# Batch 0 of a fused attention and two-layer kernel: its own states loaded first, products of the identity, another order of the plan

## The chip, the cores and the metric

One core of a Trainium2 chip. The metric is device time in microseconds; the time of a kernel is the median of its runs. Matrix products run on TensorE (PE), elementwise work on VectorE (DVE), ScalarE (ACT) and GpSimd (POOL); transfers are issued from the queues of SyncE (SP) and ScalarE.

## The reference

```python
# x (8, 8, 512, 64), state (8, 8, 32, 64), w_in (512, 2048), w_out (2048, 512)
scores  = x @ state.T / 8;  a  = softmax(scores);  xread = a  @ state
scores2 = state @ x.T / 8;  a2 = softmax(scores2); sread = a2 @ x
y = concat([xread, sread], axis=2)          # per batch 512 token rows and 32 state rows
y = y.transpose(0, 2, 1, 3).reshape(4352, 512)
h = y @ w_in
g = where(h > 0, h, exp(min(h, 0)) - 1)     # ELU
out = g @ w_out
```

The weights arrive as 64-bit floats and are turned into 32-bit ones on the core.

## The kernel before

Eight batches run one after the other, then the state rows of all of them. Batches 1 to 7 form g from M = (states times w_in) and the softmax, sixteen feature blocks each, and multiply g by w_out in a form with fewer products (`Strassen`), while the attention of the next batch is woven in. Batch 0 is different: in it the weights are still arriving and being converted. Its steps stand in `plan`, an order written out by hand, and PE, SP, ACT, DVE and POOL each keep the order in which the plan names their instructions. From batch 1 on DVE, ACT and POOL may be reordered by the scheduler.

The names of the plan, with the engine of each; g counts two halves of the heads, k the weight blocks, f the sixteen feature blocks of 128:

- `kT` (PE) transposes the states, `kTc` (DVE) copies them to `kT`, which every product with states reads.
- `x:b.i` (PE) transposes half of x, `xc:b.i` (ACT) copies it. `sc:b` (PE) are the scores, 16 records, in banks 6 and 7.
- Softmax over tokens: `mx` (DVE) maximum, `ae` (ACT) exponential, `sd` (DVE) reciprocal of the sum, `sT` (PE) transposition, `sTc` (ACT) its copy, `sr` (PE) product with x, `src` (ACT) scaled copy.
- Softmax over states: `tr` (DVE) transposes the scores, `tm` (DVE) maximum, `ps` (POOL) subtraction, `te` (ACT) exponential, `su` (DVE) sum and reciprocal, `pm` (POOL) multiplication, `tt` (DVE) transposition to `aT`.
- `w:k.1` (ACT, three instructions) and `w:k.2` (DVE, four) convert weight block k of 32; blocks 0 to 3 are the first quarter of w_in, 4 to 7 the second, 8 to 11 the first quarter of w_out, 12 to 15 the third of w_in, 16 to 19 w_out, 20 to 23 w_in, 24 to 31 w_out.
- `M:0.c.h` (PE) is half a quarter of M, `Mc` (ACT) its copy; `M:1.0` and `Mc:1.0` are those of batch 1.
- `F:f` (PE) is h for block f, in bank 4 or 5; `R:f` (ACT) its exponential, `E:f` (DVE) writes g; `O:f` (PE) adds g times w_out to banks 0 to 3. At the end ACT and DVE copy these banks to `o_sb`; batch 1's third F goes to bank 3 when DVE has emptied it.

`kT`, `x`, `sc`, `M`, `sT` and `sr` all use banks 6 and 7, each after the copy of the one before. A product in 32-bit floats leaves two records on PE, a transposition one.

`fetch` issues the load of the next weight block, 512 KB, on SP. It is called six times ahead of the plan, once at `kTc` and then at the end of each `w:k.2`; after the last block it loads x of batch 1. A load waits until its place in `work` is free, eleven places that the weight blocks, the states `s_sb` and the transposed probabilities share in turn. The eight semaphores of the loads are also used in turn, so that a ninth load waits for the first to land:

```python
raw_states = load_states()          # eight loads, four on SP, four on ACT
load_x(0, [sync, scalar])           # four loads of 256 KB
for k in range(NRAW - 1):           # NRAW = 7
    fetch()
```

All instructions but a few are recorded at line 100, the helper through which the engines are called, and are told apart by their tiles.

Of the kernel before, what the change touches and what calls it, by code (L numbers as in the profile page):

```python
# [10 lines left out]
FP32 = mybir.dt.float32  # L11
# [14 lines left out]
def kernel(  # L26
# [15 lines left out]
    B, H, S, D = x.shape  # L42
    NS = state.shape[2]
    DM, DF = moe_w_in.shape
    P = 128
    R = S // P
    NP = H // 2
    G = 2
# [4 lines left out]
    NRAW = 7  # L53
# [11 lines left out]
    def pool(name, bufs, **kw):  # L65
        return ctx.enter_context(tc.tile_pool(name=name, bufs=bufs, **kw))

    cpool = pool("const", 1)
# [4 lines left out]
    work = pool("work", NRAW + 4)  # L73
# [11 lines left out]
    def bank(i):  # L85
        return psum[:, i]

    def pair(i):

        return psum[:, i : i + 2]  # L90
# [3 lines left out]
    class InOrder:  # L94
# [10 lines left out]
    tensor, sync, vector, scalar, gpsimd = (  # L105
        InOrder(e) for e in (nc.tensor, nc.sync, nc.vector, nc.scalar, nc.gpsimd)
    )
    matmul = tensor.matmul

    def transpose(out, in_):  # L110


        for t in range(2):
            rows = slice(t * 64, (t + 1) * 64)
            tensor.transpose(out[:, t], in_[rows], ident[rows, rows], tile_position=(t * 64, 0))
# [4 lines left out]
    ident = cpool.tile([P, P], FP32, name="ident")  # L120
# [6 lines left out]
    kT = cpool.tile([P, B, P], FP32, name="kT")  # L127
# [3 lines left out]
    x_t, st, m_t = {}, {}, {}  # L131

    def load_x(b, engines):
        x_t[b] = xpool.tile([P, R, DM], FP32, name="x_sb")
        x_v = x[b].rearrange("h (p r) d -> p r h d", r=R)
        for r in range(R):
            engines[r % len(engines)].dma_start(
                out=x_t[b][:, r].rearrange("p (h d) -> p h d", d=D), in_=x_v[:, r]
            )

    def load_states():
        raw = work.tile([P, B, G, D], FP32, tag="w", name="s_sb")
        s_v = state.rearrange("b (m c) n d -> m c n b d", c=G)
        for m in range(NP):
            for c in range(G):
                (sync, scalar)[c].dma_start(out=raw[m * NS : (m + 1) * NS, :, c], in_=s_v[m, c])
        return raw

    def turn_states(raw):
        ps = st["k_ps"] = pair(6).rearrange("p t (b q) -> p t b q", q=64)  # L150
        for b in range(B):
            transpose(ps[:, :, b], raw[:, b].rearrange("p c d -> p (c d)"))

    def load_weights(src):
        _, n, k = src.shape
        raw = work.tile([P, n, k], moe_w_in.dtype, tag="w", name="raw")
        sync.dma_start(out=raw, in_=src)
        return raw
# [39 lines left out]
    def load_w_in(c, k):  # L198

        h, n = divmod(k, 2)  # L200
        rows = slice(2 * n, 2 * n + 2)
        cols = slice(c * 512 + h * 256, c * 512 + (h + 1) * 256)
        return w_in[:, 2 * c + h, rows], load_weights(w_in_v[:, rows, cols])

    def load_w_out(fo):
        raw = load_weights(w_out_v[:, fo : fo + 1])
        return w_out[:, fo : fo + 1], raw
# [178 lines left out]
    def max_part(fo, e, ps):  # L386
        vector.scalar_tensor_tensor(
            out=g_all[:, fo, : ps.shape[-1]], in0=e, scalar=-1.0, in1=ps,
            op0=ALU.add, op1=ALU.max,
        )  # L390
# [247 lines left out]
    shape = [P, 3, FO // 4, P]  # L638
# [50 lines left out]
    def first_batch():  # L689

        plan = """
            kT kTc x:0.0 xc:0.0 w:0.1 x:0.1 xc:0.1 w:0.2 w:1.1 sc:0 mx:0.1 w:2.1 tr:0.1 tr:0.0
            tm:0.1 w:3.1 tm:0.0 ps:0.1 mx:0.0 w:1.2 ps:0.0 ae:0.1 ae:0.0 te:0.1 sT:0 sd:0.0 sd:0.1
            te:0.0 su:0.1 sTc:0 su:0.0 pm:0.1 w:4.1 M:0.0.0 w:3.2 pm:0.0 Mc:0.0.0 w:7.1 sr:0 tt:0.1
            tt:0.0 w:4.2 F:0 src:0 w:8.1 w:2.2 F:1 R:0 w:5.1 E:0 M:0.0.1 w:8.2 Mc:0.0.1 R:1 F:2  # L700
            w:5.2 w:9.1 O:0 E:1 w:10.1 w:9.2 R:2 F:3 w:10.2 w:6.1 M:0.1.0 O:1 E:2 Mc:0.1.0 w:6.2 R:3
            w:12.1 E:3 F:4 w:7.2 w:11.1 O:2 w:12.2 w:13.1 R:4 w:11.2 M:0.1.1 F:5 w:14.1 w:13.2 O:3
            R:5 Mc:0.1.1 E:4 w:16.1 E:5 w:14.2 F:6 w:17.1 M:0.2.0 w:16.2 F:7 R:6 w:15.1 E:6 O:4
            w:17.2 Mc:0.2.0 w:18.1 w:15.2 F:8 R:7 w:18.2 O:5 w:21.1 E:7 R:8 w:21.2 M:0.2.1 w:19.1
            O:6 E:8 w:23.1 w:19.2 Mc:0.2.1 F:9 w:23.2 w:24.1 O:7 w:25.1 w:24.2 w:20.1 w:25.2 F:10
            R:9 O:8 w:20.2 w:22.1 E:9 R:10 w:22.2 M:0.3.0 w:26.1 F:11 E:10 O:9 Mc:0.3.0 w:26.2 R:11
            w:27.1 E:11 M:0.3.1 w:29.1 w:27.2 F:12 O:10 R:12 w:29.2 Mc:0.3.1 w:30.1 E:12 F:13 w:31.1
            w:30.2 O:11 R:13 w:31.2 w:28.1 E:13 x:1.0 w:28.2 F:14 xc:1.0 x:1.1 R:14 F:15 xc:1.1 E:14
            sc:1 R:15 O:12 mx:1.0 mx:1.1 ae:1.0 tr:1.0 ae:1.1 tr:1.1 tm:1.0 sT:1 tm:1.1 ps:1.0 O:13
            sd:1.0 sTc:1 sd:1.1 E:15 ps:1.1 te:1.0 su:1.0 te:1.1 pm:1.0 su:1.1 sr:1 pm:1.1 tt:1.0  # L710
            O:14 src:1 tt:1.1 M:1.0 O:15 Mc:1.0
        """.split()
        make_identity(nc, ident)
        o_ps = [bank(c) for c in range(R)]
        order = [lambda k=k: load_w_in(0, k) for k in range(4)]
        for c in range(1, FC + 1):
            if c < FC:
                order += [lambda c=c, k=k: load_w_in(c, k) for k in range(4)]
            order += [lambda fo=fo: load_w_out(fo) for fo in range(4 * c - 4, 4 * c)]
        w, h, e = [], {}, {}  # L720

        def fetch():
            if len(w) < len(order):
                w.append(order[len(w)]())
            elif 1 not in x_t:
                load_x(1, [sync])
                for c in range(FC):
                    k = slice(2 * c, 2 * c + 2)
                    sync.dma_start(out=w_in_mem[:, k], in_=w_in[:, k])

        raw_states = load_states()
        load_x(0, [sync, scalar])
        for k in range(NRAW - 1):
            fetch()
        groups = {
            "mx": column_max, "tr": turn_scores, "ae": column_exp, "tm": row_max,
            "ps": row_subtract, "te": row_exp, "su": row_sum, "pm": row_scale,
            "tt": turn_tokens, "sd": column_total,
        }
        whole = {  # L740
            "sc": scores, "sT": turn_state, "sTc": copy_state, "sr": state_read,
            "src": keep_read,
        }
        for step in plan:
            name, _, num = step.partition(":")
            num = [int(i) for i in num.split(".") if i]
            if name == "kT":
                turn_states(raw_states)
            elif name == "kTc":
                vector.tensor_copy(out=kT.rearrange("p b (t q) -> p t b q", t=2), in_=st["k_ps"])  # L750
                fetch()
            elif name in groups:
                groups[name](*num)
            elif name in whole:
                whole[name](*num)
            elif name == "w":
                (convert_1, convert_2)[num[1] - 1](*w[num[0]])
                if num[1] == 2:
                    fetch()
            elif name == "F":  # L760
                h[num[0]] = ffn1(0, num[0])
            elif name == "R":
                e[num[0]] = exp_part(h[num[0]])
            elif name == "E":
                max_part(num[0], e[num[0]], h[num[0]])
            elif name == "O":
                ffn2_row(o_ps, num[0])
            elif name == "x":
                turn_x(*num)
            elif name == "M":  # L770
                make_m(*num)
                if len(num) == 2:
                    make_m(1, 1, first=4)
            elif name == "xc":
                copy_x(*num)
            else:
                assert name == "Mc", step
                if len(num) == 3:
                    copy_half(*num)
                else:  # L780
                    for g in range(G):
                        copy_m(*num, g, scalar.copy)
        for g in range(G):
            copy_m(1, 1, g, scalar.copy)
        for i in range(2):
            o_sb = opool.tile([P, 2, DM], FP32, tag="o", name="o_sb")
            for c in range(2):
                (scalar.copy, vector.tensor_copy)[c](out=o_sb[:, c], in_=o_ps[2 * i + c])
            store(0, i, o_sb)
# [90 lines left out]
```

## Time and profile before

| | us |
|---|---|
| median of 5 runs | 763.6 |
| lowest, highest | 763.21, 764.36 |
| the profiled execution | 764.36 |
| its span | 762.5 |
| busy in the span: PE, DVE, ACT, POOL | 730.2, 467.1, 312.2, 35.1 |
| chain that ended last | PE 90%, DVE 6%, DMA 1%, ACT 1% |

The times in a trace count from the start of the span. A line of the timeline merges neighbouring instructions of one form: start, time that they took together, engine, tiles (out<-in), shapes, number, and in brackets the idle time of the engine before them with what ended it. A line of the windows gives a stretch, its length, busy time and instructions of PE, PEld (weight loads), DVE, ACT and POOL, the granted share of the PE clock, the busy share of the DMA engines and their GB/s.

### The profile page before, as it was taken

The numbers are of one execution on the slowest core, as the hardware profiler recorded it, in microseconds if no ns is written. First come the engines' busy times: TensorE is split into PE (matmuls) and PEld (weight loads), VectorE is DVE, ScalarE is ACT, GpSimd is POOL, SyncE is SP. The second block draws the span as 40 slices with busy tenths as digits, with TensorE's granted clock in tenths as the row PEclk, the third lists the DMA queues.
The fourth block names the chain that finished last, engine by engine and source line by source line (L and its number), as shares of the span: only waits on it lengthen the run. The fifth ranks groups of instructions, "written<-read, shape, count | busy, mean of one in ns | idle before, by whom it ended". The sixth has DMA issues, their size and how long they took to land.

```text
span 762.5 us, 11358 instructions
## 1 busy us (share of the span) xinstructions
PE 730.2 (96%) x4640; PEld 504.4 (66%) x4640; DVE 467.1 (61%) x855; ACT 312.2 (41%) x575; POOL 35.1 (5%) x38
## 2 busy tenths in 40 slices
PE   3599999899999999999999999999999999999996
PEld 1234444357964798468946795479746994699885
DVE  2999979757336673567555763667356745556230
ACT  3799874553136311642055303631164206410420
POOL 0200002002000200001000200020001100000000
PEclk9899999999999999999999999999999999999999
DMA  9556810402212221214030221222122003003001
GB/s 282 214 194 214 287 51 1 110 1 111 56 56 110 112 56 56 111 47 119 30 138 1 111 57 60 106 111 57 56 110 83 31 28 138 1 1 139 28 1 28
DMA packets 49172, 66.79 MB, mean 88 GB/s; under 512 B 36832, under 2 KB 36832, under 8 KB 45280
## 3 DMA queue, kind: packets, MB, share of 16 engines
q1 hardware_dynamic: 45952, 65.28, 25.2%
q10 hardware_dynamic: 3168, 0.79, 0.5%
q8 instruction: 36, 0.59, 0.3%
q14 instruction: 16, 0.13, 0.1%
HBM read 52.95 MB, written 13.11 MB: 87 GB/s over the span
## 4 chain that ended last, share of the span: by engine, by line
PE 90%; DVE 6%; DMA 1%; ACT 1%; issue 0%; ACTq 0%; DVEq 0%
PE ps L100 90%; DVE t_w L100 1%; DVE w_in L100 1%; DMA x_sb<-in_x_dram 1%; DVE total_t L100 1%; DVE s L100 0%; DVE g_all L100 0%; DVE w_out L100 0%; DMA s_sb<-in_state_dram 0%; ACT raw L100 0%; DVE top L100 0%; ACT e_sb L100 0%; DVE aT L100 0%; DVE m_sb L100 0%; DVE top_t L100 0%; DVE o_sb L100 0%
## 5 line engine op out<-in xcount | busy, mean ns | idle before, releaser
L100 PE MATMUL ps<-aT,m_sb 128*128 128x512 f32 x512 | 229.1, 601 | 6.7 <-DVE aT L100 3.3
L100 PE MATMUL ps<-w_out,g_all 128*128 128x256 f32 (+2 forms) x1088 | 234.7, 367 | 0.7
L100 PEld LDWEIGHTS ps<-w_out,g_all 128*128 128x128 f32 x1088 | 175.6, 191 | 54.4 <-issue 35.9
L100 PEld LDWEIGHTS ps<-aT,m_sb 128*128 128x128 f32 x512 | 96.2, 192 | 129.8 <-issue 117.0
L100 ACT ACTIVATE e_sb<-ps 128x512 f32<-128x512 f32 (+1 forms) x144 | 82.5, 573 | 224.1 <-PE ps L100 206.3
L100 DVE SCALAR_TENSOR_TENSOR g_all<-e_sb,ps 128x512 f32<-128x512 f32 (+1 forms) x144 | 94.3, 656 | 116.5 <-ACT e_sb L100 116.5
L100 DVE TENSOR_TENSOR o_sb<-o_sb,ps 128x128 f32<-128x128 f32 (+2 forms) x170 | 52.8, 310 | 76.1 <-PE ps L100 74.4
L100 PE MATMUL ps<-t_w,s 128*128 128x256 f32 (+1 forms) x480 | 89.3, 338 | 0.0
L100 ACT ACTIVATE e_sb<-e_sb 128x512 f32<-128x512 f32 (+1 forms) x144 | 87.3, 606 | 4.6
L100 PEld LDWEIGHTS ps<-t_w,s 128*128 128x128 f32 x480 | 77.1, 191 | 7.3 <-DVE o_sb L100 0.2
L100 ACT COPY o_sb<-ps 128x512 f32<-128x512 f32 (+2 forms) x52 | 21.3, 424 | 121.8 <-PE ps L100 114.7
L100 ACT ACTIVATE raw<-raw 128x512 f32<-128x512 uint32 x64 | 43.6, 681 | 1.0
L100 POOL TENSOR_TENSOR t_sb<-t_sb,top_t 128x512 f32<-128x512 f32 x16 | 17.7, 1109 | 534.2 <-DVE top_t L100 534.2
L100 DVE TENSOR_TENSOR s<-s,g_all 128x512 f32<-128x512 f32 (+1 forms) x36 | 32.1, 896 | 14.4 <-PE ps L100 14.2
L100 DVE TENSOR_TENSOR g_all<-g_all,s 128x512 f32<-128x512 f32 (+1 forms) x36 | 31.9, 886 | 9.6 <-PE ps L100 9.6
L100 PE MATMUL ps<-w_in,kT 64*32 64x512 f32 (+1 forms) x576 | 33.6, 554 | 0.0
L100 DVE TENSOR_TENSOR g_all<-g_all 128x512 f32<-128x512 f32 (+1 forms) x36 | 32.2, 895 | 0.5
L100 PE MATMUL ps<-t_w,g_all 128*128 128x128 f32 (+1 forms) x240 | 32.1, 282 | 0.0
L100 DVE TENSOR_TENSOR s<-g_all 128x512 f32<-128x512 f32 (+1 forms) x36 | 31.6, 895 | 0.5
L100 PE MATMUL ps<-w_in,s 128*128 128x128 f32 x240 | 30.7, 275 | 0.0
L100 PEld LDWEIGHTS ps<-t_w,g_all 128*128 128x128 f32 x240 | 29.8, 192 | 0.5
L100 DVE TENSOR_REDUCE top<-ps 128x1 f32<-128x512 f32 x16 | 11.0, 686 | 29.1 <-PE ps L100 29.1
(78 smaller groups left out, 576.4 us busy)
## 6 DMA issues: line engine op xcount, KB each, us to landing
w_in<-w_in_mem SPq DMA_DIRECT2D x26, 1024.0 KB, 5.8
raw<-in_moe_w_in_dram SPq DMA_DIRECT2D x16, 512.0 KB, 5.5
raw<-in_moe_w_out_dram SPq DMA_DIRECT2D x16, 512.0 KB, 3.8
out_dram<-o_sb SPq DMA_DIRECT2D x16, 512.0 KB, 2.6
x_sb<-in_x_dram SPq DMA_DIRECT2D x30, 256.0 KB, 4.5
w_in_mem<-w_in SPq DMA_DIRECT2D x4, 1024.0 KB, 6.6
x_sb<-in_x_dram ACTq DMA_DIRECT2D x2, 256.0 KB, 6.0
out_dram<-o_sb SPq DMA_DIRECT2D x8, 64.0 KB, 1.7
```

What stands on the lines that cost most here:

```text
L100: ins = getattr(self.engine, name)(*args, **kw)
```

## The change

The states of batch 0 are loaded alone, in two loads ahead of x, into a tile of their own; `kT` and `kTc` deal with them alone. The states of batches 1 to 7 are loaded in eight loads on SP at the start of the 13th fetch, that is behind twelve weight blocks; the new steps `kU` and `kUc` transpose and copy them after O:4. Seven fetches stand ahead of the plan instead of six and one at `kTc`. The new step `Z:n` makes n products of the 128x128 identity with itself into bank 3, which nothing reads; 14 follow the scores, 8 the transposition `sT`, 3 the products `sr`. The plan has another order.

```diff
@@ -138,18 +138,34 @@
                 out=x_t[b][:, r].rearrange("p (h d) -> p h d", d=D), in_=x_v[:, r]
             )
 
-    def load_states():
-        raw = work.tile([P, B, G, D], FP32, tag="w", name="s_sb")
-        s_v = state.rearrange("b (m c) n d -> m c n b d", c=G)
-        for m in range(NP):
-            for c in range(G):
-                (sync, scalar)[c].dma_start(out=raw[m * NS : (m + 1) * NS, :, c], in_=s_v[m, c])
+    state_v = state.rearrange("b (m c) n d -> c m n b d", c=G)
+
+    def load_states(b0, b1, engines=None):
+
+        shape = [P, b1 - b0, G, D]
+        if b0 == 0:
+            raw = cpool.tile(shape, FP32, name="s_first")
+        else:
+            raw = work.tile(shape, FP32, tag="w", name="s_sb")
+        for c in range(G):
+            if b0 == 0:
+                engines[c % len(engines)].dma_start(out=raw[:, 0, c], in_=state_v[c, :, :, 0])
+                continue
+            for m in range(NP):
+                sync.dma_start(
+                    out=raw[m * NS : (m + 1) * NS, :, c], in_=state_v[c, m, :, b0:b1]
+                )
         return raw
 
-    def turn_states(raw):
-        ps = st["k_ps"] = pair(6).rearrange("p t (b q) -> p t b q", q=64)
-        for b in range(B):
+    def turn_states(raw, b0, b1):
+        ps = st["k_ps"] = pair(6)[:, :, : (b1 - b0) * 64].rearrange("p t (b q) -> p t b q", q=64)
+        for b in range(b1 - b0):
             transpose(ps[:, :, b], raw[:, b].rearrange("p c d -> p (c d)"))
+
+    def copy_states(b0, b1):
+        vector.tensor_copy(
+            out=kT[:, b0:b1].rearrange("p b (t q) -> p t b q", t=2), in_=st["k_ps"]
+        )
 
     def load_weights(src):
         _, n, k = src.shape
@@ -693,22 +709,23 @@
 
 
 
+
         plan = """
...
+            kT kTc x:0.0 xc:0.0 x:0.1 w:0.1 xc:0.1 w:0.2 w:1.1 sc:0 Z:14 tr:0.0 tr:0.1 w:2.1 tm:0.0
+            tm:0.1 ps:0.0 w:3.1 mx:0.1 mx:0.0 ps:0.1 w:1.2 ae:0.0 te:0.1 ae:0.1 sd:0.0 su:0.1 w:5.1
+            M:0.0.0 sd:0.1 pm:0.1 w:3.2 Mc:0.0.0 te:0.0 sT:0 w:4.1 tt:0.1 su:0.0 sTc:0 w:5.2 pm:0.0
+            w:8.1 Z:8 sr:0 tt:0.0 src:0 w:2.2 Z:3 F:0 w:6.1 F:1 w:8.2 R:0 M:0.0.1 R:1 E:0 Mc:0.0.1
+            E:1 O:0 w:9.1 w:4.2 w:10.1 w:9.2 F:2 w:7.1 w:6.2 M:0.1.0 F:3 R:2 w:7.2 Mc:0.1.0 O:1
+            w:11.1 E:2 R:3 w:10.2 M:0.1.1 w:12.1 F:4 w:11.2 Mc:0.1.1 O:2 R:4 E:3 w:14.1 w:12.2 F:5
+            w:13.1 E:4 w:14.2 O:3 R:5 w:16.1 E:5 w:13.2 F:6 w:17.1 w:16.2 M:0.2.0 R:6 F:7 w:18.1
+            w:17.2 O:4 Mc:0.2.0 w:18.2 w:20.1 kU w:15.1 E:6 O:5 w:20.2 w:21.1 w:15.2 w:19.1 F:8 kUc
+            O:6 R:8 w:21.2 R:7 w:22.1 E:7 M:0.2.1 E:8 F:9 w:19.2 Mc:0.2.1 w:23.1 M:0.3.0 F:10 w:22.2
+            w:24.1 O:7 w:23.2 R:9 Mc:0.3.0 E:9 w:25.1 w:24.2 M:0.3.1 F:11 Mc:0.3.1 R:10 w:25.2 O:8
+            R:11 E:10 w:26.1 E:11 F:12 w:29.1 w:26.2 O:9 w:30.1 w:29.2 w:27.1 F:13 w:30.2 w:28.1
+            O:10 w:27.2 R:13 R:12 w:28.2 x:1.0 w:31.1 O:11 E:12 E:13 xc:1.0 w:31.2 x:1.1 O:12 xc:1.1
+            sc:1 O:13 mx:1.1 mx:1.0 ae:1.1 tr:1.0 ae:1.0 tr:1.1 sd:1.0 sT:1 tm:1.0 tm:1.1 ps:1.0
+            F:14 sTc:1 sd:1.1 ps:1.1 te:1.0 sr:1 R:14 su:1.0 F:15 te:1.1 pm:1.0 E:14 src:1 su:1.1
+            O:14 R:15 tt:1.0 pm:1.1 E:15 tt:1.1 M:1.0 O:15 Mc:1.0
         """.split()
         make_identity(nc, ident)
         o_ps = [bank(c) for c in range(R)]
@@ -720,6 +737,8 @@
         w, h, e = [], {}, {}
 
         def fetch():
+            if len(w) == 12 and len(raw_states) == 1:
+                raw_states.append(load_states(1, B))
             if len(w) < len(order):
                 w.append(order[len(w)]())
             elif 1 not in x_t:
@@ -728,9 +747,9 @@
                     k = slice(2 * c, 2 * c + 2)
                     sync.dma_start(out=w_in_mem[:, k], in_=w_in[:, k])
 
-        raw_states = load_states()
+        raw_states = [load_states(0, 1, [sync, scalar])]
         load_x(0, [sync, scalar])
-        for k in range(NRAW - 1):
+        for k in range(NRAW):
             fetch()
         groups = {
             "mx": column_max, "tr": turn_scores, "ae": column_exp, "tm": row_max,
@@ -744,11 +763,13 @@
         for step in plan:
             name, _, num = step.partition(":")
             num = [int(i) for i in num.split(".") if i]
-            if name == "kT":
-                turn_states(raw_states)
-            elif name == "kTc":
-                vector.tensor_copy(out=kT.rearrange("p b (t q) -> p t b q", t=2), in_=st["k_ps"])
-                fetch()
+            if name in ("kT", "kU"):
+                turn_states(raw_states[name == "kU"], *((0, 1) if name == "kT" else (1, B)))
+            elif name in ("kTc", "kUc"):
+                copy_states(*((0, 1) if name == "kTc" else (1, B)))
+            elif name == "Z":
+                for i in range(num[0]):
+                    matmul(bank(3)[:, :P], ident, ident, start=True, stop=True)
             elif name in groups:
                 groups[name](*num)
             elif name in whole:
```

On PE the order from `sc:0` to the second O is now: scores, Z:14, M:0.0.0, sT, Z:8, sr, Z:3, F:0, F:1, M:0.0.1, O:0, F:2, M:0.1.0, F:3, O:1. Before it was: scores, sT, M:0.0.0, sr, F:0, F:1, M:0.0.1, F:2, O:0, F:3, M:0.1.0, O:1. On PE at the end of batch 0 the order is now: scores of batch 1, O:13, sT, F:14, sr, F:15, O:14, M:1.0, O:15; before: scores, O:12, sT, O:13, sr, O:14, M:1.0, O:15. On DVE E:14 now comes after three of the six sums `t_w`; before it came ahead of the scores. The order of batches 1 to 7 and of the state rows is the same on every engine.

More of the change, by code (lines that the diff above doesn't have):

```diff
@@ L696, in first_batch @@
         plan = """
[L697 to L711, printed above, removed]
+            kT kTc x:0.0 xc:0.0 x:0.1 w:0.1 xc:0.1 w:0.2 w:1.1 sc:0 Z:14 tr:0.0 tr:0.1 w:2.1 tm:0.0
+            tm:0.1 ps:0.0 w:3.1 mx:0.1 mx:0.0 ps:0.1 w:1.2 ae:0.0 te:0.1 ae:0.1 sd:0.0 su:0.1 w:5.1
```

## The prediction

> **What bounds the kernel now.** I read the page's busy line and waits first, then TensorE in order of time over batch 0, then the chain over batch 0's end.
>
> ```profile
> PE 730.2 (96%) x4640; PEld 504.4 (66%) x4640; DVE 467.1 (61%) x855; ACT 312.2 (41%) x575; POOL 35.1 (5%) x38
> ```
>
> Busy time, share of the span, instructions. Who TensorE waited for (us in total, times, longest):
>
> ```profile
> PE ps L100 <- DMA s_sb<-in_state_dram: 5.6, 2, 4.6
> PE ps L100 <- ACT a_s L100: 5.1, 1, 5.1
> PE ps L100 <- DVE aT L100: 3.3, 1, 3.3
> PE ps L100 <- ACT xT L100: 2.8, 2, 1.7
> PE ps L100 <- DMA x_sb<-in_x_dram: 2.6, 2, 2.1
> ```
>
> TensorE is busy 96% of the span, so only its 32 us of idle time and its slow matmuls can be won. These waits all lie in the first 41 us:
>
> ```profile
> 11.80 0.80 PE L100 MATMUL ps<-ident,x_sb 64*128 64x64 f32 x10 [2.06 <-DMA x_sb<-in_x_dram]
> ...
> 16.56 1.96 PE L100 MATMUL ps<-xT,kT 64*32 64x512 f32 x16 [1.67 <-ACT xT L100]
> 23.61 1.97 PE L100 MATMUL ps<-ident,a_s 128*128 128x128 f32 x8 [5.09 <-ACT a_s L100]
> ...
> 28.55 1.10 PE L100 MATMUL ps<-x_sb,aT_s 128*32 128x64 f32 x64 [1.20 <-ACT m_sb L100]
> 32.99 5.94 PE L100 MATMUL ps<-aT,m_sb 128*128 128x512 f32 x8 [3.34 <-DVE aT L100]
> ...
> 40.45 1.98 PE L100 MATMUL ps<-aT,m_sb 128*128 128x512 f32 x4 [0.92 <-ACT m_sb L100]
> ```
>
> First number: start; second: duration; in brackets: idle time before and its releaser. x's last quarter lands at 11.8, the scores run at 16.56, F:0 and F:1 at 32.99, and there they take 5.94 us; the same eight records take 3.60 at 131.34. The clock's rows (last but two columns) say why:
>
> ```profile
> 24.00:28.00 4.00, 3.35 (x24) 1.57 (x22) 3.76 (x12) 3.53 (x8) 0.57 (x1) 1.00 0.35 124
> 28.00:32.00 4.00, 1.10 (x64) 0.94 (x64) 3.86 (x7) 3.94 (x10) 1.53 (x2) 0.84 0.07 26
> 32.00:36.00 4.00, 3.01 (x4) 1.47 (x5) 3.83 (x9) 0.61 (x2) 0.00 (x0) 0.50 0.76 257
> 36.00:40.00 4.00, 3.53 (x21) 1.02 (x20) 3.21 (x6) 3.13 (x6) 0.00 (x0) 0.81 0.77 233
> ```
>
> Half speed runs from about 30.7 to 37.5, after a stretch (28 to 32) with 1.10 us of work in four. From 40.45 to 134.9 TensorE does not stop. Then batch 1's F:2 waits 1.80 us for VectorE, which has to empty bank 3 first:
>
> ```profile
> 134.28 0.60 DVE o_sb L100
> ...
> 136.08 0.61 DVE o_sb L100
> ...
> 136.74 3.27 PE ps L100 x7
> ```
>
> After 136.74 the two programs have the same order on every engine, so the gain is what F:2 of batch 1 gains. The profiled execution took 764.36 us (span 762.5, 1.9 around it), the highest of five; the median is 763.6. I carry the difference from one to the other unchanged.
>
> **Step 1: loads.** Before, eight state loads of 64 KB are issued from 0.73 to 2.2, and the x loads wait for their semaphores: issues at 3.05, 3.31, 4.07, 4.41. After, two loads of 32 KB go first and x is issued by about 1.7. All of it moves in 256-byte rows, at 219 and 182 GB/s in the rows of 2 to 4 and 4 to 6 us. State and x (1.57 MB) become first state and x (1.11 MB): 0.46 MB less at 0.2 MB/us is 2.3 us. The last x load of before also took 7.3 us to land, against 4.5 to 5.0 for the others, because it was issued last, at 4.41, and ran against weights; of these 2.3 us over the median I take 0.6 to 1.5 as won, since both queues now end together. So x lands 2.9 to 3.8 earlier; I take 3.45, at 8.3. This 1:1 shift goes through turning, copying and scores: VectorE starts on the scores at 15.25 instead of 18.69. The small kT copy (1.23 us before) and its table load on ScalarE lie before 8.3 and cost nothing. Weight block 0, next on SP's queue, landed with x before (11.7) and should again; it is used 1.8 us later.
>
> **Step 2: VectorE from the scores to E:0.** Work in the new order, by spacing of the same rows in before: two transposes 1.22, two tm 1.16, two mx 1.59, w:1.2 2.25 (as 54.02 to 56.27), sd 0.26, su 1.08, sd 0.25, w:3.2 2.95 (as 22.66 to 25.61 and 28.71 to 31.64, where a GpSimd operation ran beside a block), tt 0.61, su 1.08, w:5.2 2.95, tt 0.61. Sum 16.0, so F:0 can start at 31.25 instead of 32.99. Half of step 1's gain is gone: three blocks stood before the last tt, now four (w:5.2 is new). ScalarE keeps ahead: w:5.1 ends at 23.1, te:0.0 at 24.1 and is needed at 26.5. Then w:2.2 and w:8.2 (4.5) and E:0 (0.6) end at 36.35; R:0 on ScalarE is over at 34.3.
>
> **Step 3: identity products.** 25 products are 50 records. Products of 128x128 with own weights run at 134 ns each back to back (32.1 us over 240), at half speed 246 ns (the 128x128 turns above, 1.97 us for 8). Z:14 follows the scores at 15.1 and takes 3.8 to 6.9 us, over by 22; M:0.0.0 needs ae:0.1 (21.3) and w:1.2 (21.5), and its copy stands on ScalarE behind w:5.1, until 23.1. So Z:14 is hidden, its cover 1 us. The score transposition runs 23.7 to 24.8, Z:8 to 26.9, state reads to 28.2 (they need sTc, 27.05), Z:3 to 29.0, 2.2 us before F:0. At half speed all through they would end at 32.2, 1 us late. What they buy is F:0 and F:1 in 3.6 instead of 5.94: if work is judged in windows (30.7 to 37.5 looks like two of 3.4 us), the worst placed one now holds 1.26 us in 3.4 (37%); the one that lost the speed held 1.1 (33%), and one around the 1.80 us wait at 135 held at least 47% and kept it. I take full speed, nearer to neither row, because only a third of the possible placements are that bad. The Trainium skill ("TensorE: Matmul & The Clock Gate", Part 1) lowers the clock after an idle window of about 3.4 us. The row lost it with a third of the window busy, so the rule is too mild here. By the rule F:0 and F:1 are safe and the sum below stands; by the row they may take up to 5.94, and the sum be 1.45 smaller.
>
> F:0, F:1 and M:0.0.1 end at 35.45; O:0 then waits 0.95 for E:0, to 36.4.
>
> **Step 4: from O:0 to the scores of batch 1.** Before, 40.45 to 113.39 is 72.94 of unbroken work: F:2 to F:15, O:0 to O:11, six M, two turns of x, scores. After, it has one O more (3.53), two F fewer (3.53) and the other states' 14 turns (16 took 0.65): 73.5, so scores end at 109.9. Does VectorE keep up? From 36.35: E:1 to E:13 at 0.6, 26 blocks at 2.25, the kU copy 1.1, 2.0 of sums for later batches: 69.4, at 105.8, 4 us in hand; ScalarE's 24 blocks at 1.84, 12 R at 1.16 and copies end earlier still. I followed the plan step by step by these spacings; the nearest calls are O:8 for w:24.2 (even), M:0.3.1 for w:23.2 (0.4) and O:4 for w:16.2 (0.9). I price local waits at 0 to 1 us and take 0.
>
> The other states' eight loads now stand on SP's queue between blocks 11 and 12, with issues of 0.45 each: 3.6 us for every load behind. Block 12 is issued at 39.4, lands by 43 to 45 and is converted at 46.6. Block 22 takes the buffer of these states and waits, blocks 23 to 25 behind it, for the 14 turns after O:4 (66.7); with 3.3 to 5.5 us to landing it is there at 72, used at 74.3. Both are hidden; past that cover each us is a us on ScalarE, which has slack.
>
> **Step 5: the tail.** VectorE starts mx:1 at 110.05. Before it ran 23.13 from there without a stop to the second o_sb; after, E:14 also lies inside: 23.73. F:2 at 133.85. On TensorE the same tail now has two waits: E:14 stands behind three t_w sums, 10.1 after mx, so O:14 waits 1.9 (118.85 to 120.8), and the second M of batch 1 waits 0.4 for E:15; F:1 ends at 133.7. The t_w sums take 1.13 alone and 1.94 beside GpSimd: 0.8 either way.
>
> **Sum.** 136.74 - 133.85 = 2.9 us: 3.45 from the loads, less 1.7 for w:5.2's place, plus 2.34 for F:0 and F:1 at full speed, plus the 0.92 wait of F:2 that goes, less the 0.95 of O:0 that comes: 4.05 at the start of the long stretch (40.45 against 36.4); less 0.55 for the turns and 0.6 for E:14. So 764.36 - 2.9 = 761.5 for the profiled execution and 760.7 for the median.
>
> **Rivals.** Differences under 0.2% (1.5 us), about what a measurement of this kernel can tell from no change, count as the same.
> Half of it: x lands only 1.5 to 2 us earlier since weights now follow it closer, or F:0 and F:1 stay slow (O:0 at 37.85). Either leaves 1.0 to 1.5: 762.1 to 762.6. For: the clock fell at 33% busy. Against: 50 records of filling.
> The order eats the gain: if x lands no earlier, w:5.2, the turns and E:14 make it 0.6 slower, 764.2. For: x's rate, not its issue, is a limit. Against: 0.46 MB really leave its front.
> Slower: the identity products do not overlap with their weight loads, for each loads 128 columns and writes the same place. A record is then 282 + 191 = 473 ns (the means of a 128x128 product and of a weight load): Z:14 13.2 us, M:0.0.0 at 28.4 instead of 21.5, Z:8 and Z:3 10.4, F:0 at 42 and F:2 7 us later than before: 770.7. It gives no gain from 0.33 us a record, and a loss over 0.2% from 0.36. Against: 128x128 products of before overlap fully and show no idle time.
>
> **Numbers.** Forecast (759.6 to 762.0) 0.62; half 0.15, of which a third still under 762.1; gain eaten 0.08; slower 0.15, from the products or a queue that I took as covered. Faster 0.68, same 0.17, slower 0.15. Range: down to 759.2 (x at 7.9, tail sums 0.8 shorter, a wait less), up through the half case and the eaten gain to 763.8.
>
> **What would show it.** x's last turn near 8.3; F:0 near 31.3 and eight records in 3.6; O:0 near 36.4; scores of batch 1 end near 110; F:2 of batch 1 near 133.9 after o_sb. Wrong if identity records exceed 0.25 us, if F:0 waits for them, if TensorE shows waits between 37 and 110 (for w_in, w_out or raw), or if the clock is 0.5 at F:0.

## The result and the profile after

The changed kernel takes 762.34 us (median of 25 runs, 760.8 to 764.78), the kernel before beside it 763.38 (45 runs, 762.52 to 764.46). The ratio is 0.9988, 95% interval 0.9983 to 0.9994: about 0.9 us faster. The forecast was a gain of 2.9; what came is the rival "half of it", and less than the 0.2% that I had set as the bound of a difference. The profiled execution took 762.81 (span 760.7), 1.55 less than the one of before.

The busy line of the page after, and then its waits of TensorE (total, times, longest):

```profile
PE 736.1 (97%) x4690; PEld 510.4 (67%) x4690; DVE 465.1 (61%) x856; ACT 312.2 (41%) x575; POOL 35.4 (5%) x38
```

```profile
PE ps L100 <- DMA x_sb<-in_x_dram: 3.8, 4, 2.0
...
PE ps L100 <- DVE aT L100: 2.8, 1, 2.8
PE ps L100 <- DVE g_all L100: 1.9, 3, 1.3
...
PE ps L100 <- ACT a_s L100: 1.0, 2, 0.6
```

There are 50 records more, those of the identity products, and 5.9 us more of busy time; the 5.1 us wait for `a_s` is filled by them down to 1.0. The wait for `aT` ahead of F:0 went only from 3.3 to 2.8. New is `g_all`. TensorE over batch 0, the same view as in the prediction:

```profile
9.11 0.80 PE L100 MATMUL ps<-ident,x_sb 64*128 64x64 f32 x10 [0.39 <-DMA x_sb<-in_x_dram]
...
15.74 4.82 PE L100 MATMUL ps<-ident 128*128 128x128 f32 x28
...
28.36 0.94 PE L100 MATMUL ps<-ident 128*128 128x128 f32 x6
32.08 5.40 PE L100 MATMUL ps<-aT,m_sb 128*128 128x512 f32 x8 [2.78 <-DVE aT L100]
...
38.00 3.70 PE L100 MATMUL ps<-w_out,g_all 128*128 128x512 f32 x8
```

x's last part is there at 9.11 (forecast 8.3), F:0 starts at 32.08 (31.25), F:0 and F:1 take 5.40 (3.6), O:0 starts at 38.00 without a wait (36.4). The windows after, the clock in the last column but two:

```profile
28.00:32.00 4.00, 1.30 (x38) 1.02 (x26) 3.84 (x8) 3.74 (x8) 1.05 (x1) 1.00 0.61 120
32.00:36.00 4.00, 3.92 (x5) 1.65 (x6) 3.79 (x9) 0.39 (x1) 0.00 (x0) 0.57 0.86 288
```

By rows of 1 us the clock is half from 32.4 to 35.8, one stretch of 3.4 us where before had two (30.7 to 37.5). In the 3.41 us ahead of 32.4 TensorE worked 0.63: Z:3 was over at 29.30, and F:0 came 2.8 us later. The end of batch 0, the same view:

```profile
111.09 1.09 PE L100 MATMUL ps<-xT,kT 64*32 64x512 f32 x16
...
122.67 3.70 PE L100 MATMUL ps<-w_out,g_all 128*128 128x512 f32 x8 [1.32 <-DVE g_all L100]
...
131.71 10.46 PE L100 MATMUL ps<-aT,m_sb 128*128 128x512 f32 x24
```

The wait of 1.80 for `o_sb` is gone: 24 records run through, so F:2 starts one F:0 and F:1 later (eight records, spaced 3.53 in all), at 135.24 (136.74 before, forecast 133.85). In its place O:14 waits 1.32 for E:14.

### The profile page after: what moved, and what is told of

Same layout as the page of the kernel before. It is cut to its first block, busy times and chain, and to the rows that moved or that the text cites. A ratio compares the mean times of both kernels' runs of the same rounds, so it can differ in the third digit from the quotient of the medians.

```text
span 760.7 us, 11453 instructions
## 1 busy us (share of the span) xinstructions
PE 736.1 (97%) x4690; PEld 510.4 (67%) x4690; DVE 465.1 (61%) x856; ACT 312.2 (41%) x575; POOL 35.4 (5%) x38
## 4 chain that ended last, share of the span: by engine, by line
PE 85%; DVE 11%; ACT 1%; DMA 1%; issue 0%; ACTq 0%; DVEq 0%
PE ps L100 85%; DVE w_in L100 5%; DVE w_out L100 2%; DVE g_all L100 1%; DMA x_sb<-in_x_dram 1%; DVE t_w L100 1%; DVE s L100 0%; DVE top L100 0%; DVE total_t L100 0%; ACT e_sb L100 0%; DVE m_sb L100 0%; DVE top_t L100 0%; ACT xT L100 0%; DVE t_sb L100 0%; ACTq L100 0%
## 5 line engine op out<-in xcount | busy, mean ns | idle before, releaser
L100 DVE TENSOR_TENSOR g_all<-g_all 128x512 f32<-128x512 f32 (+1 forms) x36 | 32.3, 896 | 0.5
L100 PE MATMUL ps<-w_in,s 128*128 128x128 f32 x240 | 30.7, 275 | 0.0
```

The source lines that it names most:

```text
L100: ins = getattr(self.engine, name)(*args, **kw)
```

## The experiments

Beside the traces of before and after there are twelve more. They can be compared at one mark, the start of the product M of batch 2: the time of the profiled execution less this mark is 620.4 to 620.7 us in thirteen of the fourteen (621.3 in "order alone", where 0.4 more than elsewhere lies outside the span). So nothing behind the first 144 us differs by more than about 0.3 us. All in us; x's last part is the last group of turns that waited for x's load, and the ratio is to the runs of before on the same chip. "Before, once more" is a single execution. Medians of two versions come from different sets of runs, some on different chips; the ratios allow for that.

| version | x's last part | F:0 starts | F:0 and F:1 take | scores of batch 1 | M of batch 2 | profiled run | median | ratio (95%) |
|---|---|---|---|---|---|---|---|---|
| before | 11.80 | 32.99 | 5.94 | 112.30 | 143.80 | 764.36 | 763.38 | |
| before, once more | 10.20 | 31.64 | 6.23 | 111.07 | 142.57 | 763.13 | | |
| after | 9.11 | 32.08 | 5.40 | 111.09 | 142.11 | 762.81 | 762.34 | 0.9988 (0.9983-0.9994) |
| loads only | 8.98 | 30.17 | 6.19 | 110.34 | 141.84 | 762.52 | 763.01 | 0.9995 (0.9987-1.0004) |
| before + products | 10.78 | 33.55 | 3.60 | 110.96 | 142.46 | 763.00 | 762.93 | 0.9994 (0.9986-1.0003) |
| after, no products | 8.76 | 31.75 | 5.90 | 111.24 | 142.25 | 762.62 | 763.55 | 1.0001 (0.9993-1.0010) |
| after, 12 for 3 | 8.57 | 31.77 | 3.70 | 109.48 | 140.50 | 760.90 | 761.40 | 0.9978 (0.9970-0.9986) |
| order alone | 10.58 | 33.55 | 5.40 | 111.55 | 142.56 | 763.86 | 763.65 | 1.0001 (0.9992-1.0010) |
| loads + products | 10.40 | 31.58 | 3.70 | 110.64 | 142.14 | 762.87 | 761.82 | 0.9983 (0.9974-0.9992) |
| earlier aT | 9.03 | 29.33 | 3.70 | 109.43 | 140.45 | 760.81 | 761.26 | 0.9973 (0.9964-0.9982) |
| x first, states on two queues | 7.88 | 33.06 | 3.70 | 110.77 | 141.78 | 762.18 | 762.44 | 0.9988 (0.9979-0.9997) |
| x first, states on SP | 7.54 | 31.89 | 3.60 | 109.10 | 140.12 | 760.48 | 760.56 | 0.9962 (0.9948-0.9975) |
| the same, earlier aT | 7.68 | 29.52 | 3.60 | 108.97 | 139.98 | 760.36 | 760.14 | 0.9957 (0.9944-0.9969) |
| the same, earlier scores | 7.89 | 28.66 | 3.70 | 105.34 | 138.84 | 759.20 | 759.18 | 0.9942 (0.9928-0.9956) |

**Theory** after the result: x comes early, but by 1.5 to 2 us only; the order gives a part of that back; and the filling is too short, since it ends three products after `sr` while F:0 waits for VectorE. **Rival 1**: the new order is what costs, and products are of no use. **Rival 2**: the middle, from O:0 to the scores of batch 1, is set by VectorE or by the weights, so that nothing won ahead of it counts.

### The loads alone

```diff
 # loads as in the change; the plan of before, without Z
-            w:17.2 Mc:0.2.0 w:18.1 w:15.2 F:8
+            w:17.2 Mc:0.2.0 kU w:18.1 w:15.2 kUc F:8
```

> The new loads (own states of batch 0 first, the others behind block 12, kU after M:0.2.0's copy) in the old order of the plan, no identity products. Theory (the loads shift all work before F:0 one to one, the new order gives much of it back): x's last turn near 9.1 as in the changed kernel, F:0 near 30.3 (32.99 less 2.7), F:0 and F:1 still at half speed for most of their time, F:2 of batch 1 near 134.6 (2.7 less 0.6 for the turns): about 2 us faster than before, so 1 us faster than the changed kernel. Rival (the new order is what gains, the loads do little): within 0.5 us of before.

Measured: ratio 0.9995, a gain of 0.4 us with an interval that holds zero. The 2 us of the theory did not come; the time is that of the rival, though the trace shows the shift of x. The timeline of TensorE with the loads alone:

```profile
8.98 0.80 PE L100 MATMUL ps<-ident,x_sb 64*128 64x64 f32 x10 [0.17 <-DMA x_sb<-in_x_dram]
...
30.17 6.19 PE L100 MATMUL ps<-aT,m_sb 128*128 128x512 f32 x8 [2.53 <-DVE aT L100]
...
67.74 0.65 PE L100 MATMUL ps<-ident,s_sb 64*128 64x64 f32 x14
```

How much earlier x is depends on which trace of before it is held against, so before was profiled once more:

> The kernel before once more, unchanged: one more look at where x lands with the old loads. Theory (x lands at about 10.6 to 10.8 with the old loads, as in the two other traces with them, and the 11.80 that the forecast started from was the late end): last turn of x between 10.3 and 11.2. Rival (11.8 is the rule and the other two were early): 11.6 or later.

The timeline of TensorE in that second look at before:

```profile
10.20 1.06 PE L100 MATMUL ps<-ident,x_sb 64*128 64x64 f32 x12 [1.65 <-DMA x_sb<-in_x_dram]
...
31.64 6.23 PE L100 MATMUL ps<-aT,m_sb 128*128 128x512 f32 x8 [2.52 <-DVE aT L100]
```

With the old loads x's last part comes at 10.20, 10.58, 10.78 and 11.80 in four traces, a little earlier than I expected of the rerun; with the new loads at 8.57, 8.76, 8.98, 9.03, 9.11 and 10.40 in six. The means are 10.84 and 9.14: 1.7 us. 11.80, from which the forecast started, is the latest of all. Against the second look the loads bring 1.22 at x, 1.47 at F:0, then lose 0.65 to the turns of the other states in the middle of unbroken work (the line at 67.74), and 0.73 is left at the scores and at M of batch 2. That is what the loads are worth in a profile.

### The products

First the products without the rest, twelve ahead of F:0 in the kernel before:

```diff
+            ... Z:12
             F:0
```

> The kernel before with one step more: 12 identity products directly ahead of F:0, in its 3.3 us of idle time. Theory (the clock falls because the stretch ahead of F:0 is nearly empty): no 0.50 in the clock's rows from 32 to 36, F:0 and F:1 in 3.6 to 4.2 instead of 5.94 us; the next matmuls then wait for VectorE's E:0 and w:8.2, so 1.5 to 2 us faster than before. Rival (the products do not count as work for the clock): F:0 and F:1 at 5.4 to 5.9, same time as before. Second rival (they hold F:0 up): F:0 later than 33.2 and slower than before.

The timeline of TensorE, before with these products:

```profile
29.38 4.34 PE L100 MATMUL ps<-ident 128*128 128x128 f32 x24
33.55 3.60 PE L100 MATMUL ps<-aT,m_sb 128*128 128x512 f32 x8
```

F:0 and F:1 run at full speed, but F:0 has no wait for `aT` any more: it waits for the products, 24 of them in 4.34 us, part of it at half speed. VectorE had `aT` at 31.92, so they hold F:0 up by 1.6 and win 2.3: ratio 0.9994, not the 1.5 to 2 us of the theory. Then the change without its products:

```diff
-            ... sc:0 Z:14 tr:0.0 ... w:8.1 Z:8 sr:0 ... w:2.2 Z:3 F:0
+            ... sc:0 tr:0.0 ... w:8.1 sr:0 ... w:2.2 F:0
```

> The changed kernel without its 25 identity products. Theory: the products kept the clock full for M:0.0.0, the transposition and the state reads, none of which is on the path to F:0, but the 2.8 us of idle time ahead of F:0 made F:0 slow all the same; without them two slow windows instead of one, F:0 and F:1 in 5.9 instead of 5.4, so 0.3 to 0.6 us slower than the changed kernel. Rival (the products pay): 1.5 us or more slower than the changed kernel. Rival (they are in the way): faster than it.

The timeline of TensorE without products:

```profile
31.75 5.90 PE L100 MATMUL ps<-aT,m_sb 128*128 128x512 f32 x8 [2.88 <-DVE aT L100]
```

Ratio 1.0001, about 1.0 us slower than after, between the theory (0.3 to 0.6) and the rival (1.5). Besides F:0 and F:1 (5.90), M:0.0.0 takes 2.46 and `sr` 1.93 there, against 1.45 (in two pieces) and 1.14 after. The 1.0 rests on the medians: the two profiled executions are only 0.14 apart at M of batch 2, with x 0.35 earlier in the one without products. So rival 1 falls for the products. Then more of them, at the place that the profile names:

```diff
-            ... w:2.2 Z:3 F:0
+            ... w:2.2 Z:12 F:0
```

> The changed kernel with 12 identity products after the state reads instead of 3, to fill the 2.8 us of idle time ahead of F:0. Theory: clock 1.00 at F:0, F:0 and F:1 in 3.6 instead of 5.4, after which O:0 waits up to 0.9 for E:0 (VectorE has w:2.2 and w:8.2 until 36.5): O:0 at 37.0 to 37.2 instead of 38.0, 0.8 to 1 us faster than the changed kernel. Rival (the clock does not depend on this stretch): same time as the changed kernel.

The timeline of TensorE with twelve, and below it the window from 32 to 36 of the same kernel:

```profile
28.04 2.94 PE L100 MATMUL ps<-ident 128*128 128x128 f32 x24
31.77 3.70 PE L100 MATMUL ps<-aT,m_sb 128*128 128x512 f32 x8 [0.79 <-DVE aT L100]
```

```profile
32.00:36.00 4.00, 4.00 (x24) 1.39 (x23) 3.79 (x8) 1.72 (x3) 0.00 (x0) 1.00 0.93 308
```

At full speed 24 records take 2.94, 122 ns each, and leave 0.79 ahead of F:0; the clock's column stays at 1.00 and F:0 and F:1 take 3.70. 761.40, 0.9 faster than after in the medians. The clock term is real, and three products were too few.

A caution on that column: each trace lists the changes of the clock only from the first change to full speed on, and ahead of it the column shows 1.00 while the records run at half speed. A window of "loads only":

```profile
32.00:36.00 4.00, 4.00 (x7) 1.54 (x5) 3.21 (x7) 1.95 (x4) 0.00 (x0) 1.00 0.73 200
```

Seven records fill its four us. In three traces ("loads only", "after, no products" and before's second look) the records of F:0 and F:1 take 0.90 to 0.95 us each on average (neighbouring records overlap) under a column of 1.00, as long as in before (0.91), where it says 0.50; with twelve products they take 0.60. There I go by the records. The first change to full speed comes at 35.2, 36.2 and 36.8 in these three, at 32.3 in "before + products" and at 27.3 in before, but at 16.0 to 20.9 in all nine traces with products behind the scores (18.8 in after). So in the three the clock had not fallen ahead of F:0: it had not yet risen. The products behind the scores bring it up early, and those ahead of F:0 keep it up.

### The order

```diff
 # the new plan with Z, the loads of before (written as against the change)
-        raw_states = [load_states(0, 1, [sync, scalar])]
+        raw_states = load_states()
-            ... w:20.1 kU w:15.1 ... F:8 kUc O:6
+            ... w:20.1 w:15.1 ... F:8 O:6
```

> The old loads (all states ahead of x) with the new order and its 25 identity products; kU and kUc fall away. Theory: w:5.2 ahead of the last tt puts F:0 0.7 to 1 us later than in the kernel before (33.2 to 34.0, by where x lands), F:0 and F:1 in 3.6 to 5.4 by the phase of the clock, O:14 waits 1.3: medians within 0.8 us of before, on either side. x's last turn between 10.8 and 11.8, as in the two traces with these loads so far. Rival (the new order is a gain of its own): 1 us or more faster than before.

Ratio 1.0001: order and products without the loads bring nothing (F:0 at 33.55, 5.40 us, as after). And the old order with loads and products:

```diff
 # the first experiment, and
-            sc:0 ...  F:0
+            sc:0 Z:10 ...  Z:11 F:0
```

> The new loads in the old order (e1) with 10 products after the scores and 11 ahead of F:0. Theory (the products pay by the clock at F:0, not through the new order): F:0 near 30.3, F:0 and F:1 in 3.6 to 4.2, F:2 then waits up to 1.4 for ACT's copy of M:0.0.1; 1 to 2 us faster than e1, within 0.6 us of e4. Rival (they pay only with the new order): within 0.5 us of e1.

The timeline of TensorE with the old order, the new loads and products:

```profile
27.51 2.72 PE L100 MATMUL ps<-ident 128*128 128x128 f32 x22
31.58 3.70 PE L100 MATMUL ps<-aT,m_sb 128*128 128x512 f32 x8 [1.35 <-DVE aT L100]
```

0.9983, within 0.4 us of the new order with twelve products. Its trace has the late x (10.40), so the medians say more than the profile. Laid out as steps, by ratios times 763.4: the loads 0.4 faster, the order on top of them 0.5 slower, the products of the change on top of both 1.0 faster: 0.9 together. Each step is uncertain by about 0.8 us; only that of the products lies beyond it. Whether the order costs anything stays open.

### Where F:0's gain goes

F:0 waits for the second `tt`. In this version it comes earlier, and VectorE's part of block 5 stands behind O:0:

```diff
-            ... mx:0.1 mx:0.0 ps:0.1 w:1.2 ae:0.0 te:0.1 ae:0.1 sd:0.0 su:0.1 w:5.1
-            M:0.0.0 sd:0.1 pm:0.1 w:3.2 Mc:0.0.0 te:0.0 sT:0 w:4.1 tt:0.1 su:0.0 sTc:0 w:5.2 pm:0.0
-            w:8.1 Z:8 sr:0 tt:0.0 src:0 w:2.2 Z:12 F:0 ... O:0 w:9.1 w:4.2 w:10.1
+            ... mx:0.1 mx:0.0 ps:0.1 w:1.2 ae:0.0 te:0.1 ae:0.1 te:0.0 sd:0.0 su:0.1
+            M:0.0.0 sd:0.1 pm:0.1 su:0.0 pm:0.0 Mc:0.0.0 sT:0 tt:0.1 w:3.2 w:8.1 Z:6 sTc:0 sr:0
+            w:4.1 src:0 tt:0.0 w:5.1 Z:7 w:2.2 F:0 ... O:0 w:9.1 w:4.2 w:5.2 w:10.1
```

> The changed kernel with the softmax over states drawn ahead: te:0.0 directly after ae:0.1, su:0.0 and tt:0.1 ahead of w:3.2, w:5.2 from ahead of F:0 to behind O:0, 6 products after sT and 7 ahead of F:0. Theory (w:5.2's place cost F:0 1.7 us): F:0 near 30.0 instead of 32.1, F:0 and F:1 in 3.6 to 4.5, O:0 at 35.0 to 35.6 (VectorE has w:2.2, w:8.2 and E:0 first) instead of 38.0; a wait of 0.5 to 1 near M:0.1.1 for w:7.2; 1.5 to 2.4 us faster than the changed kernel. Rival (VectorE, 4 us in hand, becomes the bound in the middle): waits for w_in or w_out between 40 and 110 that give it all back, same time as the changed kernel.

The timeline of TensorE with the earlier `aT`:

```profile
29.33 3.70 PE L100 MATMUL ps<-aT,m_sb 128*128 128x512 f32 x8 [0.30 <-DVE aT L100]
...
34.52 3.70 PE L100 MATMUL ps<-w_out,g_all 128*128 128x512 f32 x8 [0.90 <-DVE g_all L100]
...
46.92 0.64 PE L100 MATMUL ps<-w_in,kT 64*32 64x256 f32 x8 [0.21 <-DVE w_in L100]
...
109.43 1.09 PE L100 MATMUL ps<-xT,kT 64*32 64x512 f32 x16
```

O:0 is 2.3 earlier than with twelve products in the change's order (36.85), although x came 0.46 later; the scores of batch 1 are only 0.05 earlier (109.48), and the medians are 0.14 apart. What was moved behind O:0 is missing there: the second quarter of M runs at the pace at which VectorE hands over w_in (the line at 46.92), and 1.5 of the 2.3 are gone by 50. VectorE is busy 9.6 of 10 us from 37 to 97; its work from the scores to E:13 is the same in both orders. The time is 1.1 below after, where 1.5 to 2.4 was expected. An earlier F:0 that is bought with VectorE's own work is hardly a gain: 0.14 here, and 0.4 between the same two orders with x first, below.

### x ahead of the first states

What does move VectorE's start is x. First with the order of the loads turned round:

```diff
-        raw_states = [load_states(0, 1, [sync, scalar])]
         load_x(0, [sync, scalar])
+        raw_states = [load_states(0, 1, [sync, scalar])]
-            kT kTc x:0.0 xc:0.0 x:0.1        # kT in banks 6 and 7
+            x:0.0 kT xc:0.0 kTc x:0.1        # kT in banks 4 and 5
```

> The kernel with 12 products ahead of F:0 (e4), and x's loads issued ahead of the two state loads; kT goes to banks 4 and 5, between the two turns of x. Theory (the state loads take 0.72 us of SP's and 1.15 us of ScalarE's queue to issue, and x's first rows start that much later): x's loads issued at 0.73, its last turn at 7.9 to 8.3 instead of 8.6 to 9.1, 0.6 to 1 us faster than e4. Rival (the rows' rate is the limit, or the first load of a queue is slow to issue whatever it is): last turn at 8.5 or later, same time as e4.

x came at 7.88, as the theory said, yet F:0 1.3 later than with twelve products and x second, and the median is 1.0 above that version's. The timeline of ScalarE's queue in this kernel, and then that of its TensorE:

```profile
2.02 1.96 ACTq L100 DMA_DIRECT2D s_first<-in_state_dram  x1
```

```profile
12.44 0.37 PE L100 MATMUL ps<-ident,s_first 64*128 64x64 f32 x2 [3.75 <-DMA s_first<-in_state_dram]
```

The 32 KB load took 1.96 us to issue and landed 8.4 us after that, while SP's queue already moved weights. So both state loads went to SP, behind x and ahead of the weights:

```diff
-        raw_states = [load_states(0, 1, [sync, scalar])]
+        raw_states = [load_states(0, 1, [sync])]
```

> The changed kernel with twelve products ahead of F:0, x issued first, both loads of the first states behind it on SP's queue and ahead of the weights; states turned between the two turns of x. Theory (x's landing shifts everything behind it one to one, and the last run with x first lost it only through the state load on ScalarE's queue): x's last turn at 7.9 to 8.3, kT not waited for by more than 0.3, F:0 at 31.0 to 31.3 instead of 31.77, O:0 about 0.6 earlier than 36.85, scores of batch 1 at 108.8 to 109.0, and 0.5 to 0.8 us faster than the version with x second. Rival (VectorE or the weights limit the middle, as for the earlier second transposition): the scores of batch 1 stay at 109.4 or later and the time is the same within 0.3.

The timeline of TensorE with x first and the states on SP:

```profile
7.54 0.80 PE L100 MATMUL ps<-ident,x_sb 64*128 64x64 f32 x10 [0.24 <-DMA x_sb<-in_x_dram]
...
24.90 3.25 PE L100 MATMUL ps<-ident 128*128 128x128 f32 x16
...
29.11 2.94 PE L100 MATMUL ps<-ident 128*128 128x128 f32 x24
31.89 3.60 PE L100 MATMUL ps<-aT,m_sb 128*128 128x512 f32 x8
```

x is 1.03 earlier than with twelve products and x second, and `aT` was ready at 31.2, 0.5 earlier. The other half went ahead of the scores: ScalarE's second copy of x stands behind `w:0.1`, which waited 0.66 for weight block 0. F:0 did not use the 0.5: the eight products ahead of `sr` ran for the most part at half speed (3.25 us for 16 records, 1.95 in after), and the twelve behind it ended only with F:0's start. That is the cost that the prediction named for products at half speed, about 0.7 here. O:0 still came 0.5 earlier (36.35), the scores of batch 1 0.4, and the median is 760.56, 0.8 below (the profiled execution 0.4). Between the two expectations, nearer to the theory. With the earlier `aT` and fewer products behind it:

```diff
 # x's and the states' loads as in the version above, the plan of "earlier aT" with its first steps in this order
-            kT kTc x:0.0 xc:0.0 x:0.1
+            x:0.0 kT xc:0.0 kTc x:0.1
```

> The same loads (x first, first states behind it on SP) with the order in which the softmax over states comes earlier and block 5's VectorE part after O:0. Theory (the 2.3 us that this order won at O:0 was lost since block 5 came late for the second quarter of M, and VectorE's total up to there is unchanged): F:0 at 28.6 to 28.9, M:0.1.0 still waits, and the scores of batch 1 come as early as in the other order with x first, 108.8 to 109.1; time within 0.3 us of it. Rival (the weights' arrival, which does not move with x, holds block 5): the scores of batch 1 stay at 109.4.

760.14: 1.1 below the same plan with x second (0.45 in the profiled executions), and the scores at 108.97 as the theory said. F:0, expected at 28.6 to 28.9, came at 29.52 although `aT` was there at 28.3: the clock had fallen at 22.8, and the products held F:0 up again. Of the 1.35 that x is earlier than with the same plan and x second, 0.95 reached the scores of batch 0 and 0.46 those of batch 1. So the middle takes over a part of what comes from x. That rival 2 holds for gains that push VectorE's work back is what the two orders suggest; no run separates it further.

The runs of each of the versions with x first lie within 0.2 to 0.5 us (5 to 11 runs, the fourth follows below), those of after within 4.0 (25), of twelve products with x second within 3.3 (12), and of every other version with x second within 1.7 to 2.7. That the order of the loads sets the spread is shown by that; that it is x's load on ScalarE's queue running against weights is only argued, from its landing (8.57 to 10.40 with the same loads), and these 1.8 us are less than half of the 4.0. The smaller spread is also why the medians gain more from x first than the profiled executions do.

### The tail

VectorE is idle for 4.2 us ahead of the scores of batch 1, and E:14 stands behind its work on them.

```diff
-            O:10 w:27.2 R:13 R:12 w:28.2 x:1.0 w:31.1 O:11 E:12 E:13 xc:1.0 w:31.2 x:1.1 O:12 xc:1.1 sc:1 O:13
+            x:1.0 O:10 w:27.2 R:13 R:12 w:28.2 xc:1.0 x:1.1 w:31.1 O:11 E:12 E:13 xc:1.1 w:31.2 sc:1 O:12 O:13
```

> The last version (x first, earlier softmax over states), and at the end of batch 0 the two turns of x of batch 1 and its scores each stand one O earlier on TensorE, so that O:12 and O:13 follow the scores. VectorE was idle for 4.2 us before these scores, and E:14 stood behind its work on them, so that O:14 waited 1.32. Theory (the tail is set by VectorE's work from the scores to E:14, and by TensorE alone from there on): scores of batch 1 at 105.3 instead of 108.97, VectorE's idle time before its first maximum about 0.5 instead of 4.2, no wait of O:14, F:0 of batch 1 at 128.3 instead of 129.59, and 1.1 to 1.4 us faster, about 758.9. Rival (another wait takes its place: R:14, which comes after F:14 and so no earlier, or the o_sb copies ahead of F:2): gain at most 0.4.

The timeline of TensorE with the earlier scores, and then that of VectorE:

```profile
105.34 1.09 PE L100 MATMUL ps<-xT,kT 64*32 64x512 f32 x16
...
119.40 3.70 PE L100 MATMUL ps<-w_out,g_all 128*128 128x512 f32 x8 [0.36 <-DVE g_all L100]
...
128.44 7.89 PE L100 MATMUL ps<-aT,m_sb 128*128 128x512 f32 x18
```

```profile
106.61 0.69 DVE L100 TENSOR_REDUCE top<-ps 128x1 f32<-128x512 f32 x1 [0.63 <-PE ps L100]
```

VectorE's idle time ahead of its first maximum is 0.63. The median is 759.18, 1.0 lower: O:14's wait falls from 1.32 to 0.36 and F:0 of batch 1 comes at 128.44 instead of 129.59. The rest of the wait stays: four sums, not three, now stand ahead of E:14 (VectorE's order in the trace), and VectorE waits 0.67 for ScalarE's exponential in between. The gain is 0.1 short of the 1.1 to 1.4 expected. This is the fastest version, 0.6% below before and 0.4% below after (759.18 against 762.34, medians of different sets of runs).

## Why the prediction was right in direction and short in size

By its own steps, against the profiled executions, for which the sum was made; the gain there was 1.50 at F:2 instead of 2.9.

- **Step 1, x 3.45 earlier**: 2.69 (11.80 to 9.11), and 1.7 by the means of all traces with each kind of loads, so that not even the 2.3 of bytes over rate is shown. x was assumed to be issued by 1.7; it was issued at 1.51, 1.92, 2.25 and 2.36, for the small state load costs 0.72 us of issue on SP and 1.15 on ScalarE, where a load of `s_sb` took 0.46 (1.85 for four) and 0.48. With x issued first, at 0.73 on both queues, its last part came at 7.54 to 7.89. So the term that was mis-sized, by 0.8, is x's place behind the small state loads.
- **Step 2, 16.0 us of VectorE work**: held. F:0 is late by 0.83, all of it x.
- **Step 3**: identity records overlap with their weight loads (122 ns at full speed), so the slower rival was wrong from its first line, and no product of the change delayed F:0. But F:0 and F:1 took 5.40, not 3.6: I had weighed windows with 37% of work in the worst place, and the one that came held 0.63 of 3.41 us, because the last three products ended 2.8 ahead of F:0, not 2.2. Here the forecast's own sign of being wrong, half a clock at F:0, is what the profile shows. 1.8 lost, of which 0.95 came back, since E:0 was ready when F:1 ended: O:0 is 1.6 late, 0.83 from x and 0.8 from the clock. The stated alternative ("the sum be 1.45 smaller") was the right case to lead with.
- **Step 4**: no wait of TensorE from 38.0 to the scores, as said; the stretch took 74.1 instead of 73.5. 4.2 us of VectorE's time in hand, forecast 4. None of the queue costs showed.
- **Step 5**: scores to F:2 took 23.1 instead of 23.95. O:14's wait was 1.32 (forecast 1.9), and F:2 did not wait for `o_sb`, where the forecast still had VectorE's 23.73 as the limit. 0.8 better than forecast.

Sum: 2.9 - 0.8 - 0.8 - 0.6 + 0.8 = 1.5.

The second failure is not in a step but in the sentence "I carry the difference from one to the other unchanged". The profiled execution of before was the highest of the five runs then at hand, and its x, at 11.80, came 1.0 to 1.6 later than in the three other traces with the same loads. A step that moves x was thus measured from an execution in which x was worst. Before's profiled execution lies 1.0 above its median, after's 0.5: hence 1.55 in the profiles and 1.0 in the medians.

The rule of the Trainium skill that the prediction weighed ("TensorE: Matmul & The Clock Gate", Part 1: half speed after an idle window of 3413 ns) is borne out in its length: the slow stretches ahead of the long one here last 3.4 and 6.8 us, and the changes of the clock in one trace lie 3.41 us or a multiple of it apart. It is not borne out as a test of idleness. The 3.41 us ahead of a fall held 1.15 us of work in before, 0.63 after, 1.04 in "order alone", and 1.4 in the first and 1.44 in the second version with x first and states on SP (42%); no such stretch with 1.61 us (47%) or more lost the speed. Of the 1.4, 0.56 were transpositions, which by Part 4 of that page do not count as busy in the same way; the 1.44 held none. I took full speed because only a third of the places would be bad by the row; the row was the better guide.

That the state load on ScalarE's queue came last when weights were moving on the other queue agrees with "DMA: Bandwidth & Descriptors" (section on queues, rings and completion order), by which a DMA engine takes turns between queues a packet at a time, from which it would follow that a queue of small rows moves fewer bytes in its turns. The 8.4 us to landing are the row; no run here separates turns by packet from other sharing.

## What to carry to other kernels

Take a transfer's landing from several traces before a forecast rests on its being moved: the profiled execution may be the one in which it was worst. Filling for the clock first has to bring it up, and that to hold it has to reach to the instruction that it is for, and no further: in the change's order twelve products for three bought 0.9 us, and twelve that ran partly at half speed held the next product up by 1.6. An earlier start counts only if the engine that sets the pace afterwards, here VectorE, gets its own work earlier too.

## What was not expected of the hardware

- The same 24 identity records took 2.94 us at full speed and 4.34 with a part at half speed, so a filling that fits in one execution can be late in another.
- The issue of a load of 128 partitions with 256 bytes each (32 KB) took 0.72 us on SP, 1.15 on ScalarE ahead of x, and 1.96 on ScalarE behind x; a state load of 64 KB in 32 partitions took 0.46 to 0.48.
- With x issued first the spread of a kernel's runs was 0.2 to 0.5 us; with x second it was 1.7 to 4.0.
- The clock's column reads 1.00 ahead of the first change that the trace lists, while records run at half speed (0.90 to 0.95 us on average for those of F:0 and F:1 in three traces, 0.60 at full speed); the records' durations are the safer sign.
- In fourteen traces the clock first rose at 16.0 to 20.9 us with products behind the scores and at 27.3 to 36.8 without; it fell in the middle of the work only behind 3.41 us with 1.44 us of work or less.
